# New due times, DMA latency and task costs in the list schedule of a fused attention and SoLU feed-forward kernel

## The chip, the cores and the metric

The kernel runs on one core of a Trainium2 chip. The metric is device time in microseconds (us) of that core; several executions are timed and the median counts. One more execution is taken with the hardware profiler, and all rows shown here come from it.

The core's engines each run their own instruction list in order: TensorE (PE, with its weight loads shown as PEld), VectorE (DVE), ScalarE (ACT), GpSimd (POOL) and SyncE (SP), which here issues nearly all DMAs. Semaphores tie them together, so an instruction that waits holds up all that stands behind it on its engine.

## The reference

```python
scores = scale * np.matmul(q, k.transpose(0, 1, 3, 2))     # q, k, v: 4 x 8 x 768 x 64
...
scores = scores + bias[None, :, :, :]
scores = np.where(keep, scores, -1000000000.0)
...
a = a / (np.sum(a, axis=-1, keepdims=True) + 1e-09)
return np.matmul(a, v).astype(np.float32)
...
h = x @ w_in                                               # x: 3072 x 512, w_in: 512 x 1024
...
solu = h * sm
mu = np.mean(solu, axis=-1, keepdims=True)
var = np.mean((solu - mu) ** 2, axis=-1, keepdims=True)
ln = (solu - mu) / np.sqrt(var + 1e-06) * g_ln
return (ln @ w_out).astype(np.float32)
```

Four batches of eight heads go through attention. A query sees the 96 keys up to itself and the first 8 keys of the sequence; a bias falls with distance. The heads are laid side by side to 3072 tokens of width 512. A feed-forward layer follows: a product with w_in, SoLU (h times its softmax), a layer norm, and a product with w_out. The layer norm's scale cancels the softmax's sum, so that the kernel takes h times exp(h), and w_out is scaled by g_ln and centred ahead of the product.

## The kernel before, in words

Tokens come in 24 tiles of 128, six to a batch. Tile n is numbered through all batches, and token tile n of a batch with a = n mod 6 needs the keys of its own and of the tile before (with a = 0 only its own, and half the work). Every piece of work is a task, added with `add` to a planner (`Plan`, lines 22 to 100). The tasks, by their names in lines 460 to 547:

- `ql`, `qc`, `qt`, `qo`: for each batch, four head pairs and q or k: load (SP, 384 KB), cast to 16 bits (GpSimd, in batch 0 VectorE too), turn (six PE transposes into the PSUM tile pt), and copy in order of tokens (VectorE or ScalarE) into qkT.
- `vl`, `vc`: load and cast of one tile of v (256 KB; GpSimd).
- `s`, `e`, `m`, `av`, each for a half of four heads: scores (PE, tile ps), exponential (ScalarE, eb), mask (VectorE, in place), product with v (PE, tile pav). `gk` and `gv` are GpSimd's copies of the eight global keys and values into the place of the oldest ones, between one tile and the next.
- `n`, `xt`, `xc`: norm by the softmax's sum (VectorE), turn (PE, again a pt), copy to xT (VectorE).
- `h`, `he`, `u`, `ut`, `q`: product with w_in (PE, ph), its exponential (ScalarE), h times exp(h) (VectorE), transposing DMA of u (SP), sum of squares (ScalarE).
- `st`, `pw`, `o`, `os`, `w`: statistics and power (GpSimd) for two tiles, product with w_out (PE, po), scaling (ScalarE or VectorE), store (SP).
- `w_in`, `g`, `wl`, `gr`, `gm`, `gc`: loads of the weights; eight roundings of g times w_out; their mean by one PE product (pm, in po's buffer); eight centrings. No `o` runs before the last `gc`.

The planner places one task at a time. `ready` gives when a task could start on an engine: when the engine is free, its predecessors have ended (with a hop of 0.12 us if on another engine) and a buffer is there. Among the tasks within 0.15 us of the earliest it takes the one with the lowest due time and writes it to the program at once. So the planner's costs and due times set nothing but the order of each engine's list, and which engine does a task that two may do. The buffers (`rooms`, lines 204 to 208) are few in PSUM: one each for ps, pav, pt, ph and po. Before the change, due times are written out task by task in units of T = 5.4, such as

```python
add(("h", n), {"PE": 1.75}, lambda e, n=n: ffn_in(n), s + 1.5 * T,
...
add(("o", n), {"PE": 1.75}, lambda e, n=n: ffn_out(n), s + LAG * T,
```

with s = n T, and LAG = 7. A halved task's second half is due T / 2 later.

Of the kernel before, what the change touches and what calls it, by code (L numbers as in the profile page):

```python
# [21 lines left out]
class Plan:  # L22
# [8 lines left out]

    NEAR = 0.15
    DEEP = 2.5

    def __init__(self, start, hop, rooms):
        self.free = dict(start)
        self.hop = hop
        self.rooms = {r: [0.0] * n for r, n in rooms.items()}
        self.tasks, self.end, self.dma = {}, {}, 0.0

    def add(self, name, engs, emit, due, after=(), takes=(), frees=(), load=0.0, lag=0.0):

        assert name not in self.tasks, name
        self.tasks[name] = (engs, emit, due, tuple(after), takes, frees, load, lag)

    def ready(self, task, eng):
        _, _, _, after, takes, _, load, _ = task
        t = max(self.free[eng], self.dma - self.DEEP) if load else self.free[eng]
        for a in after:
            if a not in self.end:  # L50
                return None
            e, on = self.end[a]
            t = max(t, e + (0.0 if on == eng else self.hop))
# [6 lines left out]
    def run(self):  # L60
        log = []
        left = dict(self.tasks)
        for name, t in left.items():
            for a in t[3]:
                assert a in self.tasks, (name, a)
        while left:
            best = None
            cand = {}
            for name, task in left.items():
                for eng, us in task[0].items():  # L70
                    t = self.ready(task, eng)
                    if t is not None:
                        cand.setdefault(eng, []).append((t, task[2], name, us))
            for eng, c in cand.items():
                t0 = min(x[0] for x in c)
                t, due, name, us = min((x for x in c if x[0] <= t0 + self.NEAR),
                                       key=lambda x: (x[1], x[0]))
                if best is None or (t, due) < best[:2]:
                    best = (t, due, name, us, eng)
            assert best, sorted(left)  # L80
            t, due, name, us, eng = best
            engs, emit, due, after, takes, frees, load, lag = left[name]
            if len(engs) > 1:

                alt = [(x[0] + x[3], e, x[0], x[3]) for e, c in cand.items()
                       for x in c if x[2] == name]
                _, eng, t, us = min(alt)
# [3 lines left out]
            if load:  # L91
                self.dma = done = max(self.dma, done) + load
            done += lag
            for r in frees:
                heapq.heappush(self.rooms[r], done + self.hop)
            self.end[name] = (done, eng)
            log.append((t, us, eng, name))
            del left[name]
# [5 lines left out]
def kernel(  # L104
# [24 lines left out]
    T = 5.4  # L129
    LAG = 7  # L130

# [19 lines left out]
    with tc.manual_schedule():  # L151
# [35 lines left out]
        for h in range(H):  # L187
# [17 lines left out]
            start={"PE": 0.0, ve: 2.0, sc: 8.0, gp: 4.6, "SP": 0.6}, hop=0.12,  # L205
# [254 lines left out]
        add = plan.add  # L460
        BT = NA * T
        for b in range(B):
            for i, (w, pr) in enumerate(PAIRS):
                x = (b, w, pr)
                due = b * BT - (NP * 2 - i) * (0.8 * BT / 8) if b else -40.0 + 2 * i
                add(("ql", *x), {"SP": 0.3}, lambda e, x=x: load_pair(*x), due - 3 * T,
                    takes=("raw",), load=1.1, lag=1.0)
                add(("qc", *x), {gp: 0.86, ve: 0.85} if b == 0 else {gp: 0.86},
                    lambda e, x=x: cast_pair(*x, e), due - 0.5 * T,
                    after=[("ql", *x)], takes=("qkn",), frees=("raw",))  # L470
                last = [("s", NA * (b - 1) - 1, 1)] if b > 1 else []
                add(("qt", *x), {"PE": 0.43}, lambda e, x=x: turn_pair(*x), due,
                    after=[("qc", *x)] + last, takes=("t",), frees=("qkn",))
# [109 lines left out]
```

## Time and profile before

| | us |
|---|---|
| median of three timed runs | 185.64 (185.6 to 186.57) |
| the profiled execution, its time | 186.13 |
| its span, first to last instruction | 184.4 |
| TensorE busy in it | 147.2 |
| ScalarE, VectorE, GpSimd busy | 126.3, 119.1, 79.2 |
| DMA: bytes moved, mean rate | 34.85 MB, 189 GB/s |
| mean granted TensorE clock | 0.954 of full speed |

The span is shorter than the time by what lies around the instructions. An engine's busy time is the sum over its instructions; a row of the timeline gives the start in us, the length, the engine, the source line, the tile written and the tile read, the count, and in brackets the idle time ahead of it with what ended it. In the chain of waits each row is a start, a length and the work that the end of the kernel hung on then.

### The profile page before, as it was taken

How to read it: one execution, taken by the hardware profiler on the slowest of the kernel's cores; microseconds unless marked ns; L12 is line 12 of the kernel's file. 1: busy time of each engine (PE TensorE's matmuls, PEld its weight loads, DVE VectorE, ACT ScalarE, POOL GpSimd, SP SyncE). 2: the span in 40 equal slices, each digit the busy share in tenths (PEclk: the TensorE clock that was granted, in tenths of full speed). 3: DMA queues.
4: the chain of work that ended last, by engine and by line, in shares of the span. 5: the costliest groups of instructions: out<-in, count | busy, mean ns of one | idle time of the engine just before them, and what ended most of it. 6: DMA issues, size and time to landing. Idle time of an engine off the chain costs nothing.

```text
span 184.4 us, 3669 instructions
## 1 busy us (share of the span) xinstructions
PE 147.2 (80%) x1384; PEld 83.1 (45%) x1384; DVE 119.1 (65%) x219; ACT 126.3 (69%) x200; POOL 79.2 (43%) x157
## 2 busy tenths in 40 slices
PE   0337478686779799999999899799998799988581
PEld 0225346244455445555554465555544355444120
DVE  2351466656989996677855887696647677586220
ACT  2827357569984998657668877598787868777401
POOL 7241095357996587154543775350405214020110
PEclk9999999789969999999999999999999999999955
DMA  6999996989999999999999956039243344522731
GB/s 186 320 242 193 322 310 195 244 215 220 282 274 306 237 251 213 334 289 251 334 253 221 264 109 172 0 71 160 57 106 102 88 109 94 139 57 80 114 94 57
DMA packets 65138, 34.85 MB, mean 189 GB/s; under 512 B 52320, under 2 KB 60512, under 8 KB 65120
## 3 DMA queue, kind: packets, MB, share of 16 engines
q1 hardware_dynamic: 64592, 33.57, 74.5%
q0 software_dynamic: 528, 1.05, 3.4%
q8 instruction: 11, 0.18, 0.4%
q14 instruction: 7, 0.06, 0.1%
HBM read 23.07 MB, written 6.29 MB: 159 GB/s over the span
## 4 chain that ended last, share of the span: by engine, by line
PE 52%; DVE 12%; ACT 11%; issue 9%; DMA 6%; POOL 6%; SPq 1%; POOLq 0%
PE ph L349 20%; PE po L406 15%; PE pt L248 5%; PE pav L313 5%; PE ps L275 4%; DVE u L373 4%; DMA raw<-in_k_dram 4%; ACT eb L286 3%; DVE eb L300 3%; ACT qkT L256 3%; DMA uT<-u 2%; DVE qkT L256 2%; ACT sq L383 2%; DVE x L328 2%; ACT e L369 2%
## 5 line engine op out<-in xcount | busy, mean ns | idle before, releaser
L406 PE MATMUL po<-gw_sb,uT 128*128 128x512 f16 x192 | 47.8, 394 | 3.5 <-DMA uT<-u 2.6
L349 PE MATMUL ph<-w_in_sb,xT 128*128 128x512 f16 x192 | 47.6, 393 | 2.0 <-DVE xT L339 1.8
L286 ACT ACTIVATE eb<-ps 128x1024 f16<-128x1024 f32 x40 | 40.8, 1019 | 2.3 <-PE ps L275 2.1
L300 DVE TENSOR_TENSOR eb<-eb,mask 128x1024 f16<-128x1024 f16 (+1 forms) x48 | 34.3, 724 | 9.1 <-ACT eb L290 4.8
L369 ACT ACTIVATE e<-ph 128x1024 f16<-128x1024 f32 x24 | 24.6, 1025 | 21.6 <-PE ph L349 21.6
L373 DVE SCALAR_TENSOR_TENSOR u<-e,ph 128x1024 f16<-128x1024 f16 x24 | 29.1, 1214 | 5.0 <-ACT e L369 5.0
L248 PE MATMUL pt<-ident,qkn 128*128 128x128 f16 x192 | 19.0, 246 | 16.3 <-DVE qkT L256 6.9
L240 POOL CAST qkn<-raw 128x768 f16<-128x768 f32 x26 | 21.8, 847 | 17.1 <-PE pt L248 10.4
L406 PEld LDWEIGHTS <-uT 128*128 128x128 f16 x192 | 17.9, 100 | 24.7 <-DMA uT<-u 4.8
L349 PEld LDWEIGHTS <-xT 128*128 128x128 f16 x192 | 18.0, 101 | 22.7 <-issue 2.7
L383 ACT ACTIVATE sq<-u 128x1024 f16<-128x1024 f16 x24 | 25.4, 1059 | 3.9 <-DVE u L373 3.8
L275 PE MATMUL ps<-qkT 64*128 64x128 f16 x352 | 19.6, 228 | 7.0 <-ACT eb L286 5.5
L248 PEld LDWEIGHTS <-qkn 128*128 128x128 f16 x192 | 15.2, 110 | 21.1 <-issue 8.7
L416 ACT ACTIVATE osb<-po,rs 128x512 f32<-128x512 f32 x18 | 12.4, 686 | 14.3 <-issue 6.4
L313 PE MATMUL pav<-vo,eb 128*128 128x65 f16 x352 | 18.6, 197 | 2.7 <-DVE eb L300 1.5
L256 ACT COPY qkT<-pt 128x768 f16<-128x768 f16 x18 | 14.4, 799 | 8.5 <-PE pt L248 8.5
L222 POOL CAST vo<-vst 128x512 f16<-128x512 f32 x24 | 17.4, 729 | 5.9 <-DMA vst<-in_v_dram 4.0
L256 DVE COPY qkT<-pt 128x768 f16<-128x768 f16 x14 | 13.3, 953 | 9.8 <-PE pt L248 9.8
L226 POOL COPY vo<-vo 8x520 f16<-8x520 f16 x16 | 9.7, 609 | 19.6 <-PE pav L313 19.6
L313 PEld LDWEIGHTS <-eb 128*128 128x128 f16 x352 | 14.8, 100 | 7.2 <-DVE eb L300 4.8
L275 PEld LDWEIGHTS <-qkT 64*128 64x128 f16 x352 | 11.6, 97 | 13.4 <-issue 9.5
L328 DVE TENSOR_TENSOR x<-pav,rl 128x512 f16<-128x512 f32 x24 | 16.6, 692 | 0.8
(49 smaller groups left out, 110.4 us busy)
## 6 DMA issues: line engine op xcount, KB each, us to landing
raw<-in_q_dram SPq DMA_DIRECT2D x16, 384.0 KB, 5.8
raw<-in_k_dram SPq DMA_DIRECT2D x16, 384.0 KB, 5.7
vst<-in_v_dram SPq DMA_DIRECT2D x24, 256.0 KB, 5.0
out_dram<-osb SPq DMA_DIRECT2D x24, 256.0 KB, 2.5
w_out<-in_moe_w_out_dram SPq DMA_DIRECT2D x4, 512.0 KB, 5.0
w_in_sb<-in_moe_w_in_dram POOLq DMA_DIRECT2D x1, 1024.0 KB, 9.8
uT<-u SPq DMA_TRANSPOSE x24, 3.4
g_sb<-in_moe_g_ln_dram SPq DMA_DIRECT2D x1, 4.0 KB, 8.3
```

What stands on the lines that cost most here:

```text
L240: ENG[eng](out=t.rearrange("p a m d -> p m a d"), in_=raws.pop((b, w, pr)).rearrange("p m (a d) -> p m a d", d=D))
L248: nc.tensor.transpose(out=pt[:, a, :], in_=src[:, a].rearrange("p m d -> p (m d)"), identity=ident)
L256: ENG[eng](out=dst, in_=pts.pop((b, w, pr)).rearrange("p a t -> p t a"))
L275: nc.tensor.matmul(out=ps[:, m, slot, blk, :], lhsT=qkT[b][r, NP + pr, ts(a - blk, P)], rhs=qkT[b][r, pr, ts(a, P)], start=True, stop=True)
L286: nc.scalar.activation(out=eb.rearrange("p m s b f -> p (m s b f)"), in_=ps.rearrange("p m s b f -> p (m s b f)"), func=AF.Exp, scale=inv_ ...
L300: nc.vector.tensor_tensor(out=eb.rearrange(pat), in0=eb.rearrange(pat), in1=mk.rearrange(pat if n % NA else "p m s f -> p (m s f)"), op=AL ...
L313: nc.tensor.matmul(out=pav[:, half, ds(i * (D + 1), D + 1)], lhsT=eb[:, m, slot, blk, :], rhs=vo[:, b % 2, a - blk, 4 * half + i, :], star ...
L349: nc.tensor.matmul(out=ph[:, ds(fh * 512, 512)], lhsT=xT[:, j, :], rhs=w_in_sb[:, j, ds(fh * 512, 512)], start=(j == 0), stop=(j == NCC - 1))
L369: nc.scalar.activation(out=es[n], in_=phs[n], func=AF.Exp, accum_out=acc)
L373: nc.vector.scalar_tensor_tensor(out=us[n], in0=es.pop(n), scalar=1.0, in1=phs.pop(n), op0=ALU.mult, op1=ALU.mult, accum_out=sums(n, 1))
L383: nc.scalar.activation(out=sq, in_=us[n], func=AF.Square, scale=D_FF ** -0.5, accum_out=sums(n, 2))
L406: nc.tensor.matmul(out=po, lhsT=uT[:, c, :], rhs=gw_sb[:, c, :], start=(c == 0), stop=(c == NFC - 1))
```

## The change

The planner takes new numbers, and is told more of DMA.

- A task's due time is now T (n + D + i S), with T = 4.34, n its tile (a batch's first tile for q/k), i the half, pair or part, and D and S two numbers for its kind from a table of some 70. Batch 0, batch 1 and batches 2 and 3 have q/k kinds of their own (`ql0`, `ql1`, `ql2` and so on).
- A DMA reaches the engines 1.2 us after its issue (`SENT`) and its data are seen 0.9 us after it has landed (`SEEN`); these stand in place of a lag given with each task.
- Costs are changed by some hundredths to tenths (a turn of q/k 0.43 to 0.36, a cast of v 0.63 to 0.73, an exponential of ph 1.12 to 1.18).
- A rounding of w_out may no longer go to GpSimd, and the load of w_in no longer waits for batch 0's last cast.
- A tie between equal due times falls to the task added first.

Buffers, tiles, instructions and the arithmetic are as they were. The diff, cut:

```diff
-    def __init__(self, start, hop, rooms):
+    HOP = 0.12
...
+    SENT, SEEN = 1.2, 0.9
...
             if load:
-                self.dma = done = max(self.dma, done) + load
-            done += lag
+                self.dma = max(self.dma, done + self.SENT) + load
+                done = self.dma + self.SEEN
...
-    T = 5.4
+    T = 4.34
...
+    DUE = {
+        "ql0": -140.45, "ql0+": 3.00, "qc0": -5.55, "qc0+": 2.05, "qt0": -71.06,
...
+        "u": -79.84, "ut": -29.51, "q": -24.86, "st": -18.75, "pw": 97.28, "o": 77.23,
...
+        def due(what, n, i=0):
+
+            return T * (n + DUE[what] + i * DUE.get(what + "+", 0.0))
...
-                add(("av", n, h), {"PE": 0.13 if z else 0.26}, lambda e, n=n, h=h: av(n, h),
-                    sh + 0.5 * T,
-                    after=[("m", n, h), ("vc", n)] + ([("av", n, 0)] if h else [])
...
+                add(("av", n, h), {"PE": 0.15 if z else 0.28}, lambda e, n=n, h=h: av(n, h),
+                    n, h, after=[("m", n, h), ("vc", n)] + ([("av", n, 0)] if h else [])
...
-        add("w_in", {gp: 1.2}, lambda e: load_w_in(), -37.0, load=5.4, lag=1.0,
-            after=[("qc", 0, 1, 1)])
...
+        add("w_in", {gp: 1.2}, lambda e: load_w_in(), 0, load=5.4)
...
-            add(("gr", j), {sc: 0.62, ve: 0.62, gp: 0.75}, lambda e, j=j: gw_round(j, e),
...
+            add(("gr", j), {sc: 0.72, ve: 0.74}, lambda e, j=j: gw_round(j, e), 0, j,
```

What this does to the order is seen in the built programs. First GpSimd's list while the fourth tile is worked on; st and rs belong to the layer norm's statistics, gw_sb is the rounded w_out, vo the cast v, qkn a cast pair of q or k. Before:

```order
L260 COPY qkT<-qkT 128x4x8
L400 TENSOR_TENSOR rs<-vs,nhalf 128x2
L222 CAST vo<-vst 128x8x64
L444 TENSOR_SCALAR gw_sb<-w_out_69,g_sb 128x512 x2
L226 COPY vo<-vo 8x520
L240 CAST qkn<-raw 128x2x6x64
```

The same place in the changed program (source lines are 12 higher there):

```order
L234 CAST vo<-vst 128x8x64 x2
L238 COPY vo<-vo 8x520
L412 TENSOR_TENSOR rs<-vs,nhalf 128x2
L234 CAST vo<-vst 128x8x64 x2
L252 CAST qkn<-raw 128x2x6x64 x2
L403 TENSOR_TENSOR t_829<-st 128x4
```

The two roundings of w_out are gone from GpSimd, which casts v further ahead; ScalarE does five and VectorE three of the eight, and pm, which needs all of them, moves on TensorE from just ahead of the fifth h to between the first and the second. On SyncE the four loads of w_out move from among batch 1's loads to just behind v's first tile.

Second, TensorE's list late in the program, matrix products alone, with the buffers' numbers; ps are scores, pav the product with v, eb the exponentials (masked in place), xT the turned input of ph. Before, where eb2_2233 and eb2_2273 are the exponentials of ps_2197 (the scores ahead of this piece) and of ps_2252:

```order
L406 MATMUL po_2236<-gw_sb_71,uT_2168 128x512
...
L275 MATMUL ps_2252<-qkT_1558 128x128
...
L313 MATMUL pav_2263<-vo_67,eb2_2233 128x65
...
L349 MATMUL ph_2275<-w_in_sb_68,xT_2245 128x512
...
L313 MATMUL pav_2263<-vo_67,eb2_2273 128x65
```

In the changed program, where eb2_2131 and eb2_2182 are the exponentials of ps_2100 and ps_2143:

```order
L287 MATMUL ps_2195<-qkT_1377 128x128
...
L361 MATMUL ph_2204<-w_in_sb_68,xT_2171 128x512
...
L287 MATMUL ps_2236<-qkT_1377 128x128
...
L325 MATMUL pav_2245<-vo_67,eb2_2131 128x65
...
L325 MATMUL pav_2245<-vo_67,eb2_2182 128x65
...
L418 MATMUL po_2265<-gw_sb_71,uT_2034 128x512
```

Before, a product with v follows its own scores by one or two groups; now ps_2143, ps_2195 and ps_2236 stand between ps_2100 and the product with its exponentials.

Third, the end of TensorE's list; uT is the transposed u that the product po with w_out reads. Before:

```order
L349 MATMUL ph_2528<-w_in_sb_68,xT_2517 128x512
...
L406 MATMUL po_2566<-gw_sb_71,uT_2513 128x512
...
L349 MATMUL ph_2591<-w_in_sb_68,xT_2584 128x512
...
L406 MATMUL po_2611<-gw_sb_71,uT_2586 128x512
...
L406 MATMUL po_2637<-gw_sb_71,uT_2622 128x512
```

And in the changed program:

```order
L418 MATMUL po_2544<-gw_sb_71,uT_2366 128x512
...
L361 MATMUL ph_2565<-w_in_sb_68,xT_2522 128x512
...
L418 MATMUL po_2582<-gw_sb_71,uT_2457 128x512
...
L418 MATMUL po_2601<-gw_sb_71,uT_2524 128x512
...
L418 MATMUL po_2625<-gw_sb_71,uT_2574 128x512
...
L418 MATMUL po_2637<-gw_sb_71,uT_2612 128x512
```

The products with w_out now lag by four tiles from the start (the first one stands ahead of the fifth ph) to the end, where four follow the last ph; before, the first stood behind the seventh ph, they caught up, and two followed the last.

More of the change, by code (lines that the diff above doesn't have):

```diff
@@ L464 @@
                 x = (b, w, pr)
[L465 to L471, printed above, removed]
@@ new lines @@
+                add(("pw", g), {gp: 0.7}, lambda e, g=g: ffn_pow(g), n, after=[("st", g)])
+            add(("o", n), {"PE": 1.75}, lambda e, n=n: ffn_out(n), n,
+                after=[("ut", n)] + [("gc", j) for j in range(NFC)], takes=("o",),
+                frees=("uT",))
+            add(("os", n), {sc: 0.7, ve: 0.75}, lambda e, n=n: scale_out(n, e), n,
+                after=[("o", n), ("pw", g)], takes=("osb",), frees=("o",))
+            add(("w", n), {"SP": 0.5}, lambda e, n=n: store(n), n,
+                after=[("os", n)], frees=("osb",), load=0.75)
```

149 lines of the change are left out of this document (74 added, 75 removed), and 9 rows, old and new, of the table DUE.

## The prediction

> **What bounds the kernel now.** I read the page first, then the stages by windows, then the chain of waits in the densest stretch, then TensorE's timeline for the starts of single tasks.
>
> ```profile
> span 184.4 us, 3669 instructions
> PE 147.2 (80%) x1384; PEld 83.1 (45%) x1384; DVE 119.1 (65%) x219; ACT 126.3 (69%) x200; POOL 79.2 (43%) x157
> ```
>
> ```profile
> 0.00:26.10 26.10, 10.83 (x99) 7.99 (x100) 10.91 (x19) 13.50 (x27) 10.55 (x28) 1.00 0.97 256
> 26.10:56.60 30.50, 23.23 (x258) 14.31 (x257) 21.88 (x39) 23.44 (x35) 20.87 (x33) 0.89 0.97 248
> 56.60:169.10 112.50, 105.04 (x1007) 58.22 (x1005) 83.25 (x153) 85.36 (x132) 46.66 (x95) 1.00 0.74 171
> 169.10:184.40 15.30, 8.08 (x24) 2.59 (x24) 3.08 (x12) 4.03 (x8) 1.10 (x2) 0.67 0.41 87
> ```
>
> Each window gives length, busy time of PE, PEld, DVE, ACT, POOL, the granted clock, the DMA share and GB/s. The borders are mine: 26.1 is the start of token tile 0's first FFN product (h0), 56.6 that of h4, 169.1 that of the last, h23. Until h4 the DMA is full (0.97) and PE is not; then PE is; the end is a thin chain at a clock of 0.67.
>
> Busy time overstates PE's work, since pipelined matmuls overlap. The chain of waits shows what a task takes from start to start:
>
> ```profile
> 74.54 1.73 PE po L406 x8
> 76.26 0.22 PE pt L335 x4
> 76.49 0.24 PE pav L313 x8
> 76.73 0.33 PE ps L275 x8
> 79.13 1.73 PE ph L349 x8
> 80.86 0.35 PE pt L248 x6
> ```
>
> So o and h are 1.73 us each, a q/k turn (qt) 0.35, a half's scores 0.33, its av 0.24, a turn of x (xt) 0.22; halves of a batch's first tile take half. All 24 tiles need 24 x (2 x 1.73 + 2 x 0.33 + 2 x 0.24 + 0.22) - 2.3 for the four short tiles + 32 x 0.35 + 1.83 for the mean (gm): 126 us of the 184.4. The other 58 are waits and a slow clock. The Trainium skill, Perfetto Trace Analysis, section Identifying the Most-Contended Engine, says the same of matmul busy time: no measure of the distance to the roofline. By busy time the third window could lose at most 112.5 - 105.0 = 7.5 us.
>
> Where the waits lie follows from the starts of h1, h4, h6, h13, h16 and h23 on TensorE's timeline:
>
> ```profile
> 34.90 3.34 PE L349 MATMUL ph<-w_in_sb,xT 128*128 128x512 f16 x8 [1.09 <-DVE xT L339]
> 56.62 1.89 PE L349 MATMUL ph<-w_in_sb,xT 128*128 128x512 f16 x8
> 65.54 1.89 PE L349 MATMUL ph<-w_in_sb,xT 128*128 128x512 f16 x8
> 115.02 1.89 PE L349 MATMUL ph<-w_in_sb,xT 128*128 128x512 f16 x8
> 131.60 1.89 PE L349 MATMUL ph<-w_in_sb,xT 128*128 128x512 f16 x8
> 169.16 1.90 PE L349 MATMUL ph<-w_in_sb,xT 128*128 128x512 f16 x8 [0.52 <-DVE xT L339]
> ```
>
> I counted the tasks between these in the program's order and priced them as above. h6 to h13: 46.2 us of work in 49.5 (93%); there a backlog of thirteen o's filled every gap. h16 to h23: 31.9 in 37.6 (85%). h4 to h23 as a whole: 98.4 in 112.5.
>
> **The change part by part.** Instructions stay nearly the same; what moves is order. ScalarE gets one more q/k copy and two more roundings of gw and loses two output scalings; VectorE gets two scalings and one cast and loses one copy; GpSimd loses two roundings and a cast. Rows for these and for the loop through ph:
>
> ```profile
> L369 ACT ACTIVATE e<-ph 128x1024 f16<-128x1024 f32 x24 | 24.6, 1025 | 21.6 <-PE ph L349 21.6
> L369 ACT ACTIVATION_READ_ACCUMULATOR e<-ph 128x1 f32 x24 | 4.8, 200 | 0.0
> L373 DVE SCALAR_TENSOR_TENSOR u<-e,ph 128x1024 f16<-128x1024 f16 x24 | 29.1, 1214 | 5.0 <-ACT e L369 5.0
> L418 DVE TENSOR_SCALAR osb<-po,rs 128x512 f32<-128x512 f32 x6 | 4.5, 750 | 5.6 <-issue 2.8 <-PE po L406 1.7 <-POOL vo L222 1.1
> L441 ACT ACTIVATE gw_sb<-w_out,g_sb 128x512 f16<-128x512 f32 x3 | 2.2, 723 | 0.0
> L444 POOL TENSOR_SCALAR gw_sb<-w_out,g_sb 128x512 f16<-128x512 f32 x2 | 3.3, 1643 | 0.0
> ```
>
> VectorE's net is under 2.1 us on 119 (two scalings at 0.75 and a cast of 0.56, in a row below, less a copy), ScalarE's 0.9 on 126 (a copy of 0.81, below, and 2 x 0.72 - 2 x 0.69; its scalings last 0.69 in the last row of this part). Neither engine is full in any window, so I cost them at nothing; where VectorE or ScalarE is late, it is late for the reasons priced below. The planner's new code runs on the host: nothing.
>
> *Up to h4.* Three things change. First, the early q/k chain. VectorE's second copy stood behind a cast that waited 2.93 us for a load; ScalarE now takes that copy. After it the chain is paced by one turn (cold, 0.81) and one copy (0.81) through the single buffer t:
>
> ```profile
> 9.37 0.56 DVE L240 CAST qkn<-raw 128x768 f16<-128x768 f32 x1 [2.93 <-DMA raw<-in_k_dram]
> ```
>
> ```profile
> 11.68 0.81 ACT qkT L256
> 12.53 0.81 PE pt L248 x6
> ```
>
> That is about 1 us gained: h0 at 25.3. Second, GpSimd's two roundings go; they stood in the chain between h3 and h4:
>
> ```profile
> 46.95 3.27 POOL gw_sb L444 x2
> ...
> 54.95 1.83 PE pm L451 x8
> ```
>
> Third, all of w_out is loaded ahead of v1 and batch 1, and gm goes between h0 and h1. There it waits on PE for the eighth rounding, with the scores and q/k turns of what follows queued behind it. Walked by these durations: h0 ends at 27.8, its exponential (1.03, and 0.2 for reading its sum) and two roundings (1.45) hold gm to 30.4, PE idles 2 us, gm ends at 32.2, three turns with their copies and two score exponentials put h1 at 37; then 4.4, 5.1 and 6.0 us, the last with o0 inside, give h4 at 52.5. The short ones are the loop h, exponential, u, h through the single ph: 1.73 + 1.2 + 1.25 and hops. The walk has a full clock after h0 and lets no load be late. The window above has a clock of 0.89 and 248 GB/s, and batch 1's first pair is due on PE at 32.6 when it has been there for only about 2 us. I add 2.5: **h4 at 55.0**. Bounds: 52.5, and 60.4 if the old gap stays (56.6 + 2.1, by which h1 moves from 34.9 to 37, + 1.73 for o0).
>
> *From h4 to h23.* In after's order 19 h, 19 o, 29 full and 4 half scores, 30 full and 5 half av's, 19 xt and 15 qt stand there: 93.2 us, 5.2 less than now, since three o's lie elsewhere. The spacing of scores and av is the larger point. Now av follows its scores by one other task group and PE waits for ScalarE, then VectorE; in the new order three more score halves stand between. Going by hand through h6 to h9 with the durations above I find 15.3 us for 15.2 of work: exponential, square, mask, u and copy each end before PE asks. Such a walk leaves out late loads, so I take the best rate that PE has shown, 93.4%: 93.2 / 0.934 = 99.7. Bounds: 97% (96.0) and 84.8% (109.8). The DMA must keep up until all inputs are in. The rows of its largest loads, with KB each:
>
> ```profile
> raw<-in_q_dram SPq DMA_DIRECT2D x16, 384.0 KB, 5.8
> ...
> vst<-in_v_dram SPq DMA_DIRECT2D x24, 256.0 KB, 5.0
> ```
>
> Six tiles need 8 x 384 + 18 x 256 KB (v, uT, out) = 7.9 MB, at 250 GB/s 31.4 us, 5.2 per tile. PE's pace would be 99.7 / 19 = 5.25: they are level, so slack is what was loaded ahead.
>
> *From h23 to the end.* Now two o's follow h23, then four:
>
> ```profile
> 173.33 2.61 PE L406 MATMUL po<-gw_sb,uT 128*128 128x512 f16 x8 [2.27 <-DMA uT<-u]
> 176.83 3.57 PE L406 MATMUL po<-gw_sb,uT 128*128 128x512 f16 x8 [0.90 <-DVE osb L418]
> ```
>
> ```profile
> 180.49 0.69 ACT L416 ACTIVATE osb<-po,rs 128x512 f32<-128x512 f32 x1 [5.84 <-issue]
> ```
>
> The wait of 2.27 for the last transposes is covered by o20 and o21. But po is one buffer, so each o waits for the scaling of the one before: 1.75 (h23) + 4 x 1.73 + 3 x 0.85 + 0.3 for the end of the last, then 0.75 and the 3.2 us that now lie between the last scaling and the end: 15.5, against 15.2 now. This takes a full clock. In the rows the clock is halved in the last o (3.57 for 8); if it halves after o20 here too, three o's cost 1.75 more each: 20.7. I take the full clock, as the gaps are 0.85 and not 2.27. The Trainium skill, TensorE: Matmul & The Clock Gate, section Why this matters for your kernels, asks for gaps under about 3 us; here the clock fell after 2.27. By its rule this end stays at 15.5.
>
> **Sum.** 55.0 + 99.7 + 15.5 = 170.2 us of span. The profiled execution took 186.13 for a span of 184.4; the median, 185.64, is 1.2 above the span. So 171.4, say **171**.
>
> **The rivals.**
>
> *The pace stays.* Single buffers (s, t, ph, po) tie the engines whatever the order, and PE runs at 84.8% as it did from h16 to h23: 55.0 + 109.8 + 15.5 + 1.2 = 181.5. For it: the 83 and 85 us that VectorE and ScalarE are busy in the third window would be 83 and 86% of 99.7, in strict order. Against: the waits there were for av's mask, which now has time. 0.25.
>
> *Loads come late: slower.* GpSimd's queue is first in, first out, and the casts of v and q/k stand in it ahead of the copies of the global keys and values, for which scores and av wait. Where a cast waits for its load, PE waits too.
>
> ```profile
> POOL qkn L240 <- DMA raw<-in_q_dram: 5.3, 3, 3.2
> ...
> POOL vo L222 <- DMA vst<-in_v_dram: 4.0, 5, 1.5
> ```
>
> ```profile
> L222 POOL CAST vo<-vst x24: 606/616/1096, 14.3 to 111.7; 128x512 f16<-128x512 f32 x24
> ```
>
> The last v is cast at 111.7 now, at the latest that DMA allows; the new order would be at tile 14 by then. If PE waits 1.5 us (the longest for v) at each of the 15 tiles till then, 171.4 + 22.5 = 193.9; it is slower than before from 1.0 us a tile. Against: loads run dry only if SP waits for a u with loads behind it. 0.09.
>
> *It does nothing.* The old gap before h4 stays (60.4), PE keeps 87.4% (106.6), the end stays: 60.4 + 106.6 + 15.5 + 1.2 = 183.7, or 188.9 with the slow clock at the end. 0.05.
>
> **How the numbers follow.** The forecast has 0.54 (its own range 165 to 178: 52.5 + 96.0, and 57 + 104.9 at 88.8%, the rate of h4 to h16); better than 165 has 0.07. Faster by over 0.5%, about what a measurement of this kernel can tell: 0.54 + 0.07 + 0.25 = 0.86; same 0.05; slower 0.09. All likely cases have one sign. A range from 165 to 184 leaves out the better end (0.07), late loads (0.09) and the half of the last case that lies above 184: under 0.2.
>
> **What the new profile would show.** Right: h4 near 55 with one o done; about 5.25 us from h to h after it, PE near 9 tenths throughout; no rounding on GpSimd; four o's after h23 with gaps near 0.85 at full clock. Wrong: GpSimd's casts waiting for DMA by tens of us in all; PE waiting for VectorE or ScalarE between scores and av; a clock under 0.8 in the last window; h1 past 40 because gm waits for w_out.

## The result, and the profile after

| | median, us | runs | span of the profiled run, us |
|---|---|---|---|
| before | 185.68 | 4 (185.6 to 186.57) | 184.4 |
| after | 170.01 | 4 (169.84 to 170.58) | 168.1 |

The ratio is 0.916 (95% interval 0.912 to 0.919). The 171 us of the prediction lies 1 us above it, and the range of 165 to 184 holds it. The three terms of the sum, from the starts of h4 and h23 on TensorE's timeline:

| | before | predicted | after |
|---|---|---|---|
| up to h4 | 56.6, no o | 55.0, one o | 52.35, one o |
| h4 to h23 | 112.5, 22 o's | 99.7, 19 o's | 99.64, 19 o's |
| h23 to the end | 15.2, two o's | 15.5, four o's | 16.1, four o's |

First the page, which answers to the first two rows shown of before:

```profile
span 168.1 us, 3666 instructions
PE 142.3 (85%) x1384; PEld 78.7 (47%) x1384; DVE 118.4 (70%) x221; ACT 127.3 (76%) x201; POOL 73.8 (44%) x154
```

Then the windows between the same events, with the same columns (length, PE, PEld, DVE, ACT, POOL, granted clock, DMA share, GB/s):

```profile
0.00:24.90 24.90, 10.76 (x100) 7.74 (x100) 9.86 (x19) 15.45 (x30) 6.53 (x23) 1.00 1.00 281
24.90:52.30 27.40, 24.38 (x267) 14.22 (x266) 24.22 (x45) 23.62 (x36) 18.16 (x29) 1.00 0.97 249
52.30:152.00 99.70, 97.92 (x983) 53.03 (x984) 81.81 (x151) 82.13 (x127) 48.05 (x100) 1.00 0.84 192
152.00:168.10 16.10, 9.28 (x40) 3.71 (x39) 2.48 (x10) 6.08 (x10) 1.10 (x2) 0.96 0.52 116
```

Two numbers answer to the old windows. In the second, the column of the clock reads 1.00 and read 0.89; how far that column can be trusted there is said at the end. In the third, PE is busy for 97.9 of 99.7 us and was for 105.0 of 112.5. What ended PE's waits there is a list of two; before, the same stretch had seven kinds. First after, then before (engine, line, what it waited for, us in total, times, longest):

```profile
PE ph L361 <- DVE u L385: 0.9, 2, 0.7
PE ps L287 <- POOL qkT L272: 0.8, 2, 0.4
```

```profile
PE ps L275 <- ACT eb L286: 2.9, 6, 0.8
PE pt L335 <- DVE x L328: 1.2, 2, 1.0
PE pav L313 <- DVE eb L300: 0.9, 2, 0.5
PE ph L349 <- DVE xT L339: 0.7, 2, 0.5
PE pt L248 <- DVE xT L339: 0.5, 1, 0.5
PE pt L335 <- DVE qkT L256: 0.4, 2, 0.2
PE po L406 <- DMA uT<-u: 0.3, 1, 0.3
```

The longest of the old waits is that of scores for the exponential of the scores before them (L286), which has to read the single buffer ps first; the wait of av for the mask (L300) is 0.9 of 6.9 us.

So the 12.9 us that the middle lost are made up as follows. Three o's lie elsewhere: 5.2, at 1.73 each. The idle times in the rows of TensorE's timeline there, up to the start of h23, fell from 6.9 to 1.7: 5.2. The remaining 2.5 is work that takes less from one start to the next, av above all: that of a single half took 0.33 us on average and takes 0.26. The end, on TensorE's timeline (start, length, idle before and what ended it):

```profile
151.99 1.89 PE L361 MATMUL ph<-w_in_sb,xT 128*128 128x512 f16 x8 [0.74 <-DVE u L385]
153.72 1.89 PE L418 MATMUL po<-gw_sb,uT 128*128 128x512 f16 x8
156.43 1.89 PE L418 MATMUL po<-gw_sb,uT 128*128 128x512 f16 x8 [0.83 <-ACT osb L428]
159.09 1.89 PE L418 MATMUL po<-gw_sb,uT 128*128 128x512 f16 x8 [0.78 <-ACT osb L428]
162.12 1.90 PE L418 MATMUL po<-gw_sb,uT 128*128 128x512 f16 x8 [1.14 <-DMA uT<-u]
```

Four o's at full clock, two gaps as predicted, and a third of 1.14 that was longer and ended by a transpose, not by a scaling.

The terms of the experiments below come from the one profiled run of each kernel; for two of them (the due times alone, and o ahead of h) it took 2.7 and 4 us more than the shortest of its kernel, and the ratios, unlike the medians, leave out runs over 1.5% longer than the shortest.

### The profile page after: what moved, and what is told of

The parts are those of the page before. It is cut to its first block, busy times and chain, and to the rows that moved or that the text cites. A ratio compares the mean times of both kernels' runs of the same rounds, so it can differ in the third digit from the quotient of the medians.

```text
span 168.1 us, 3666 instructions
## 1 busy us (share of the span) xinstructions
PE 142.3 (85%) x1384; PEld 78.7 (47%) x1384; DVE 118.4 (70%) x221; ACT 127.3 (76%) x201; POOL 73.8 (44%) x154
## 4 chain that ended last, share of the span: by engine, by line
PE 44%; DMA 26%; SPq 16%; POOL 6%; issue 4%; DVE 2%; ACT 1%; POOLq 0%; ACTq 0%
PE ph L361 16%; PE po L418 14%; DMA raw<-in_k_dram 10%; DMA vst<-in_v_dram 6%; SPq L229 6%; SPq L245 6%; PE ps L287 5%; DMA uT<-u 5%; PE pav L325 5%; DMA raw<-in_q_dram 4%; SPq L447 3%; POOL qkn L252 3%; PE pt L260 2%; PE pt L347 2%; POOL vo L234 2%
## 5 line engine op out<-in xcount | busy, mean ns | idle before, releaser
L418 PE MATMUL po<-gw_sb,uT 128*128 128x512 f16 x192 | 45.3, 379 | 2.7 <-ACT osb L428 1.6
L312 DVE TENSOR_TENSOR eb<-eb,mask 128x1024 f16<-128x1024 f16 (+1 forms) x48 | 32.8, 693 | 6.1 <-ACT eb L302 4.0
L252 POOL CAST qkn<-raw 128x768 f16<-128x768 f32 x25 | 21.0, 840 | 14.7 <-DMA raw<-in_q_dram 8.6
L234 POOL CAST vo<-vst 128x512 f16<-128x512 f32 x24 | 16.5, 691 | 19.6 <-DMA vst<-in_v_dram 19.2
L260 PEld LDWEIGHTS <-qkn 128*128 128x128 f16 x192 | 14.0, 107 | 16.4 <-issue 7.4
L428 ACT ACTIVATE osb<-po,rs 128x512 f32<-128x512 f32 x16 | 11.0, 684 | 11.1 <-PE po L418 8.3
L268 ACT COPY qkT<-pt 128x768 f16<-128x768 f16 x19 | 15.2, 801 | 5.4 <-PE pt L260 5.2
L325 PE MATMUL pav<-vo,eb 128*128 128x65 f16 x352 | 16.7, 196 | 0.2 <-POOL vo L234 0.2
L268 DVE COPY qkT<-pt 128x768 f16<-128x768 f16 x13 | 12.4, 955 | 5.8 <-PE pt L260 5.8
L412 POOL TENSOR_TENSOR rs<-vs,nhalf 128x2 f32<-128x2 f32 (+1 forms) x13 | 8.9, 685 | 14.9 <-DVE vs L407 14.5
L325 PEld LDWEIGHTS <-eb 128*128 128x128 f16 x352 | 13.1, 99 | 3.1 <-issue 0.8
```

The source lines that it names most:

```text
L252: ENG[eng](out=t.rearrange("p a m d -> p m a d"), in_=raws.pop((b, w, pr)).rearrange("p m (a d) -> p m a d", d=D))
L260: nc.tensor.transpose(out=pt[:, a, :], in_=src[:, a].rearrange("p m d -> p (m d)"), identity=ident)
L268: ENG[eng](out=dst, in_=pts.pop((b, w, pr)).rearrange("p a t -> p t a"))
L312: nc.vector.tensor_tensor(out=eb.rearrange(pat), in0=eb.rearrange(pat), in1=mk.rearrange(pat if n % NA else "p m s f -> p (m s f)"), op=AL ...
L325: nc.tensor.matmul(out=pav[:, half, ds(i * (D + 1), D + 1)], lhsT=eb[:, m, slot, blk, :], rhs=vo[:, b % 2, a - blk, 4 * half + i, :], star ...
L418: nc.tensor.matmul(out=po, lhsT=uT[:, c, :], rhs=gw_sb[:, c, :], start=(c == 0), stop=(c == NFC - 1))
```

## The experiments

The theory at the start: the order that the new due times make carries the gain, by an o beside each h and by more work between scores and av; the rest of the change is calibration. The rivals: the DMA model and true costs are the gain, or GpSimd's rounding was what held the front. The table has medians of four runs or more, ratios to the kernel before on the same chip, and the terms, in us, with the number of o's in the last two. The diffs stand against the changed kernel, where nothing else is said.

| kernel | us | ratio (95%) | up to h4 | h4 to h23 (o's) | end (o's) |
|---|---|---|---|---|---|
| after | 170.01 | 0.916 (0.912 to 0.919) | 52.35 | 99.6 (19) | 16.1 (4) |
| due times alone | 176.59 | 0.949 (0.935 to 0.963) | 56.9 | 102.3 (20) | 15.7 (4) |
| all but due times | 185.78 | 1.003 (0.999 to 1.006) | 57.1 | 113.1 (22) | 13.3 (2) |
| before, GpSimd rounds nothing | 189.92 | 1.031 (1.021 to 1.041) | 52.2 | 122.7 (22) | 13.3 (2) |
| after, GpSimd rounds | 175.11 | 0.937 (0.928 to 0.945) | 54.3 | 102.1 (20) | 15.7 (4) |
| after, old DMA model | 177.74 | 0.952 (0.945 to 0.959) | 55.1 | 99.9 (18) | 21.2 (6) |
| three exponential buffers | 182.15 | 0.984 (0.974 to 0.994) | 53.2 | 100.7 (16) | 27.0 (8) |
| priority by kind | 190.92 | 1.033 (1.024 to 1.041) | 74.6 | 98.4 (18) | 16.2 (4) |
| one set for q/k | 171.98 | 0.923 (0.915 to 0.931) | 52.1 | 101.9 (19) | 16.1 (4) |
| o ahead of h | 184.47 | 0.987 (0.976 to 0.998) | 53.0 | 115.6 (21) | 15.0 (2) |
| half a v tile more | 179.74 | 0.972 (0.965 to 0.978) | 54.6 | 106.9 (19) | 16.5 (4) |
| half of v | 169.72 | 0.909 (0.902 to 0.916) | 52.7 | 98.3 (19) | 15.7 (4) |
| end in two banks | 167.56 | 0.906 (0.899 to 0.912) | 52.4 | 99.1 (19) | 13.4 (4) |

### Which part carries the gain

**Due times alone.** The table, with the costs, the DMA model and the choice of engines as before:

```diff
-    SENT, SEEN = 1.2, 0.9
+    LAGS = {"ql0": 1.0, "ql1": 1.0, "ql2": 1.0, "vl0": 1.0, "vl": 1.0, "ut": 1.5, "w": 1.5,
...
-            add(("gr", j), {sc: 0.72, ve: 0.74}, lambda e, j=j: gw_round(j, e), 0, j,
+            add(("gr", j), {sc: 0.62, ve: 0.62, gp: 0.75}, lambda e, j=j: gw_round(j, e), 0, j,
```

> The new table of due times alone: the old task costs, the old DMA model with its lags, GpSimd still offered the rounding, the load of w_in still behind the last cast of the first q/k batch. Theory: the order is the whole gain. I expect 169 to 173 us, the stretch from h4 to h23 at 99 to 102 us with an o after almost every h, and the end within 1 us of the changed kernel's 16.1. Rival (the DMA latency in the plan keeps the new order from issuing transposes and loads too late): 176 to 181 us, with PE waiting for the transposed u or for GpSimd's casts by some us in all between h4 and h23.

Measured 176.59 us (174.13 to 177.19). The middle and the end are as expected, 102.3 and 15.7, so the order does carry the larger part: 5.1 points of 8.4 (3.7 to 6.5 by the interval). But h4 comes 4.6 us later than in the changed kernel, with o0 not yet done; 1.8 us of that are h1 and h3 at a lower clock (3.33 and 2.27 us for 1.89). The rival had the right size and the wrong place: between h4 and h23 PE waits little.

**All but due times.** The complement; the due times come from the old formulas:

```diff
+        OLD = 5.4
+        def due(what, n, i=0):
+            s, b, t = n * OLD, n // NA, OLD
...
+            if what in ("s", "e", "m", "av"):
+                return s + i * t / 2 + {"s": 0.0, "e": 0.1, "m": 0.2, "av": 0.5 * t}[what]
```

> Everything of the change but the table: the new DMA model and latency, the new task costs, no rounding on GpSimd, w_in not tied to a cast; the due times come from the old formulas, with the old 5.4 us per tile. Theory: without the table the order stays that of before (attention and h keep their places, pm near h4, the o's some eight tiles behind until late), so 181 to 187 us with 109 to 113 us from h4 to h23. Rival (the plan was merely badly calibrated, and true costs and latencies would have given the gain with the old due times): 172 to 176 us.

Measured 185.78, ratio 1.003: no change, as the theory had it. The new costs and latencies do nothing for the old due times. With the new ones all that is not the table is worth the other 3.3 points. The next three runs ask what of it; no run has the new costs alone, or the earlier load of w_in alone.

**GpSimd without the rounding, in the kernel before.** Against the kernel before:

```diff
-            add(("gr", j), {sc: 0.62, ve: 0.62, gp: 0.75}, lambda e, j=j: gw_round(j, e),
+            add(("gr", j), {sc: 0.62, ve: 0.62}, lambda e, j=j: gw_round(j, e),
```

> The kernel before, with one edit: GpSimd is no longer offered the rounding of w_out, so ScalarE and VectorE do all eight; its due times, costs and DMA model stay the old ones. Theory (the order carries the gain): the rounding on GpSimd is at most a matter of the first 57 us, and h4 cannot come before pm, which stays behind it in this order; I expect 182 to 186 us, h4 between 54 and 57, the stretch from h4 to h23 at 112 us as before. Rival (the GpSimd rounding held up pm, and with it everything up to h4): h4 comes at 52 to 53 as in the changed kernel and the time is about 181. A time under 178 would refute both.

Measured 189.92: slower by 3%, which no theory had. h4 does come at 52.2, since gm now stands behind it; but the middle takes 10 us more. 1.7 of them are gm itself. PE's idle rows there come to 9.6 us for 6.9, of which 2.8 are waits for VectorE's masks; VectorE now does five of the eight roundings and did three. And the clock falls after short waits. TensorE's timeline in this run, around h6:

```profile
62.86 0.38 PE L335 MATMUL pt<-ident,x 128*128 128x128 f16 x4 [1.23 <-ACT qkT L256]
63.79 0.40 PE L275 MATMUL ps<-qkT 64*128 64x128 f16 x8 [0.54 <-ACT eb L286]
64.94 0.41 PE L313 MATMUL pav<-vo,eb 128*128 128x65 f16 x8 [0.76 <-DVE eb L300]
65.28 3.36 PE L349 MATMUL ph<-w_in_sb,xT 128*128 128x512 f16 x8
```

Three waits, none above 1.23 us, and h6 takes 3.36 us for 1.89: half the clock. h4 takes 3.44, so the two cost 3 us. The Trainium skill, TensorE: Matmul & The Clock Gate, section A second HAM failure mode: psum-queue depth-cycling, tells of a kernel in which PE idles briefly and often between groups of matmuls and its clock goes down and up again and again; the 3.36 us after these three waits agree.

**GpSimd with the rounding, in the changed kernel.**

```diff
-            add(("gr", j), {sc: 0.72, ve: 0.74}, lambda e, j=j: gw_round(j, e), 0, j,
+            add(("gr", j), {sc: 0.72, ve: 0.74, gp: 0.75}, lambda e, j=j: gw_round(j, e), 0, j,
```

> The changed kernel, with GpSimd offered the rounding of w_out again (at the old 0.75 us); the order then gives it four of the eight, early, between the copies of the global keys and the casts of v. In the run with the due times alone GpSimd had three of them, 1.56 to 1.78 us each, and h4 came at 56.9 and not at 52.4. Theory (the rounding on GpSimd made those 4.6 us): h4 at 55 to 58, 173 to 176 us, with GpSimd's casts late and the rest as in the changed kernel. Rival (the loss came from the old DMA model or the old costs): h4 at 52 to 53.5, 170 to 171.5 us.

Measured 175.11, as the theory expected; h4 at 54.3 is a little below its bounds, and o0 is not yet done there, which is 1.8 us more. The roundings by engine in this run (ns min/median/max, first and last start):

```profile
L456 POOL TENSOR_SCALAR gw_sb<-w_out,g_sb x4: 1555/1646/1745, 21.9 to 27.1; 128x512 f16<-128x512 f32 x4
L456 DVE TENSOR_SCALAR gw_sb<-w_out,g_sb x2: 479/562/646, 25.1 to 26.8; 128x512 f16<-128x512 f32 x2
```

The planner is told 0.75 us and GpSimd takes 1.65, so four of them take 3.6 us more than the plan allows. The first cast of q/k behind them starts at 31.87, and at 28.47 in the changed kernel. The order differs in other places too (h1 comes at 34.3 and not at 37.1), so how much of the loss is this queue is not split up.

**The old DMA model in the changed kernel.**

```diff
-                self.dma = max(self.dma, done + self.SENT) + load
-                done = self.dma + self.SEEN
+                self.dma = done = max(self.dma, done) + load
+            done += self.LAGS.get(name if isinstance(name, str) else name[0], 0.0)
```

> The changed kernel with the old model of a DMA in the planner (a fixed lag behind the load, no time to be sent): new due times, new costs, no rounding on GpSimd. The order then lets o0 come two tiles later and leaves six o's behind h23. Theory (the model decides where the o's stand, not when the front is done): h4 within 1.5 us of 52.4, 1.8 us less for each o that is missing up to h23, 2.7 us more for each behind it: 171.5 to 174 us. Rival (the model is what e2's front lacked): h4 at 55 to 58 and 175 to 179 us.

Measured 177.74: the rival, in place and size (e2 is the run with the due times alone). The front shows how. The plan believes that a load is there sooner than it is, and puts a cast that waits for it ahead of a copy that PE waits for. VectorE, then TensorE in this run:

```profile
9.56 0.56 DVE L253 CAST qkn<-raw 128x768 f16<-128x768 f32 x1 [2.50 <-DMA raw<-in_k_dram]
10.04 0.95 DVE L269 COPY qkT<-pt 128x768 f16<-128x768 f16 x1
```

```profile
11.04 0.80 PE L261 MATMUL pt<-ident,qkn 128*128 128x128 f16 x6 [3.12 <-DVE qkT L269]
```

This is the row of before that the prediction quoted (a cast waiting 2.93 us), back again; h0 comes at 26.7 and not at 24.9, 1.8 of the 2.8 us by which h4 is late. Another 5.1 us are at the end, where six o's stand behind h23 and not four. My theory, that the model only places the o's, fell; its price of 2.7 us for each o at the end about held, with 5.1 for two.

### What the order does

**Three exponential buffers.**

```diff
-                   "qkn": 4, "eb": 4, "x16": 2, "xT": 3, "e": 3, "u": 5, "ut": 5, "uT": LAG + 1,
+                   "qkn": 4, "eb": 3, "x16": 2, "xT": 3, "e": 3, "u": 5, "ut": 5, "uT": LAG + 1,
```

> The changed kernel, with the planner told that there are three buffers of exponentials and not four, so that the product with v can stand fewer score halves behind its scores; the buffers themselves are unchanged. By the same due times the order then leaves eight o's behind h23, not four. Theory (depth between scores and the product with v, and an o beside each h, are what took the waits away): the stretch from h4 to h23 loses three to four o's of 1.85 us (92 to 94 us if no wait comes), and waits for VectorE's masks come back by 2 to 6 us; the end takes 23 to 25 us in place of 16.1; in all 172 to 178 us. Rival (depth does not matter, the waits were those of the old order): 169 to 171 us, no PE idle row for the mask above 1 us in all.

Measured 182.15, 4 us above the theory's range and 11 above the rival's. The end is the larger part: 27.0 us, since each o behind h23 costs 2.73 us through the single po (10.9 more for four). In the middle three o's less (1.79 each, as measured in the changed kernel) should have given 94.3 and it took 100.7: 6.4 us of waits and slower steps came back, a little more than expected; 4.1 of them are idle rows. They are not the expected ones. The longest four of nine kinds:

```profile
PE ph L361 <- DVE u L385: 1.9, 4, 0.8
PE pav L325 <- POOL vo L238: 1.6, 1, 1.6
PE pt L260 <- DVE xT L351: 0.8, 2, 0.6
PE pt L260 <- ACT qkT L268: 0.6, 2, 0.3
```

No wait for the mask is in the list, so that depth helps by giving the mask time, as I had argued, is not borne out. That depth is what was lost here is not shown either. Counted on TensorE's timeline from h4 to h23, the score halves that stand between a half's scores and its av are 1.0 on average before, 2.0 in the changed kernel and 1.4 in this run; but they are 1.4 in the next run too, whose idle rows come to 1.7 us there as in the changed kernel, against 5.8 here. This run also has fewer o's to fill the middle, 16 for 19. Its loss has no single cause that is shown.

**Priority by kind.**

```diff
+        RANK = {w: r for r, w in enumerate(sorted((w for w in DUE if w[-1] != "+"),
+                                                  key=lambda w: DUE[w]))}
-            return T * (n + DUE[what] + i * DUE.get(what + "+", 0.0))
+            return 1000.0 * RANK[what] + 10.0 * n + i
```

> The changed kernel, with the due time replaced by the rank of the kind in the table (the kind with the lowest number first), then the tile, then the part; the steps and the 4.34 us per tile are gone. Theory: the table's numbers lie so far apart (from -165.81 to 97.28 tiles, and there are 24) that they act as a list of priorities and no more; I expect 168 to 174 us, the o's still one to an h. Rival (the distances and the steps are what was tuned): 176 us or more, with waits of PE between h4 and h23 of over 3 us.

Measured 190.92: the theory fell, but not where the rival said. The middle is as fast as ever (98.4 us with 18 o's). The front is 22 us later, and two rows show why. In the table the later q/k loads (9.08 and 9.34) and the v loads (12.95) lie close, so the tile's number decides between them; by rank the q/k loads go first. SyncE's queue and TensorE in this run:

```profile
45.05 0.37 SPq L245 DMA_DIRECT2D raw<-in_k_dram  x1
45.69 12.02 SPq L229 DMA_DIRECT2D vst<-in_v_dram  x7
```

```profile
55.02 1.04 PE L325 MATMUL pav<-vo,eb 128*128 128x65 f16 x16 [10.95 <-POOL vo L234]
```

v1 is issued at 45.7 and not at 14.6, behind 22 loads of q and k more, and PE stands still for 10.95 us. So on PE from h4 on the table acts as a list of priorities, and on the load queue its distances decide. The 4.34 us order nothing in the changed kernel, since they multiply every due time alike.

**One set of numbers for q/k.**

```diff
-                k_ = str(min(b, 2))
+                k_ = str(min(b, 1))
```

> The changed kernel with one set of numbers for the q/k batches 1, 2 and 3: the last two take those of batch 1, so that their transposes no longer come ahead of nearly everything and no longer wait until the last scores of the batch before. The order up to h6 hardly changes; transposes of the last two batches stand up to three earlier in the rows of PE. Theory (with room for four cast pairs, and the same loads, it hardly matters): 169.5 to 172 us. Rival (own numbers for the later batches are a part of the gain): 174 to 180 us, with PE waiting for scores or transposes between h8 and h20.

Measured 171.98, the upper end of the theory; the interval overlaps the changed kernel's. The middle is 2.2 us longer, with one wait of 1.7 for the global keys. Own numbers for the later batches are worth some 2 us in this run, and that much is not settled.

**o ahead of h.**

```diff
-        "u": -79.84, "ut": -29.51, "q": -24.86, "st": -18.75, "pw": 97.28, "o": 77.23,
+        "u": -79.84, "ut": -29.51, "q": -24.86, "st": -18.75, "pw": 97.28, "o": 40.00,
```

> The changed kernel with one number of the table changed: o from 77.23 to 40.00, so that o comes ahead of h (44.73) when both could run; two o's are left behind h23 and not four. Theory (o is the work that PE has in reserve, and is best kept back): between h4 and h23 stand two o's more (99.6 + 2 x 1.83 = 103.3 us) and PE waits for the transposed u by 1 to 4 us; the end is as long as in the kernel before, which also had two o's there (15.2 us); in all 172 to 176 us. Rival (the end is what four o's cost, 16.1 us, and falls to 12.5 with two): 167 to 170 us.

Measured 184.47 (181.27 to 185.34): the direction of the theory, 8 us above its range. The end is the expected 15.0, with the last o at half clock (3.60 us after a wait of 1.01, and one of 2.27 before it). The middle took 115.6 for the expected 103.3 plus 1 to 4. The idle rows come to 11.0 us there, for 1.7 in the changed kernel. Besides 3.2 us for the transposed u, PE waits at eleven other kinds of place; the longest four of the list:

```profile
PE po L418 <- DMA uT<-u: 3.2, 5, 1.0
PE ps L287 <- POOL qkT L272: 2.2, 1, 2.2
PE pt L260 <- DVE xT L351: 1.0, 3, 0.5
PE pt L260 <- DVE qkT L268: 0.8, 1, 0.8
```

Four o's go between h4 and h5, which come 17.5 us apart; after that no o is in reserve to fill a gap. The idle rows and the two o's make 12.9 of the 15.9 us more; where the rest goes is open.

### What bounds the kernel now

**Half a v tile more.**

```diff
+    more = const.tile([P, N_TOK // P, 4, D], FP32, name="more")
...
+            nc.sync.dma_start(out=more[:, n], in_=v[b, 0:4, ts(a, P), :].rearrange("h p d -> p h d"))
```

> The changed kernel with 24 loads more, one of 128 KB beside each tile of v, into a buffer that nobody reads: 3.15 MB on top of 34.85 MB. The output is unchanged. In the prediction the DMA of a tile (5.2 us) was level with PE's work (5.25 us). If DMA bounds the first 105 us, in which its share is 9 tenths and more, then 3.15 MB at the 260 GB/s of those windows is 12 us, and the time goes to 178 to 184 us. If PE bounds from h4 on and DMA only up to h4: up to 52 us some 12 of the 24 loads are issued, 1.6 MB or 6 us at 260 GB/s; 173 to 178 us. If DMA bounds nowhere: 170 to 171 us, only the issue time on SyncE.

Measured 179.74: the case in which DMA bounds the first 105 us. 9.8 us of span for 3.15 MB, 7.2 of them between h4 and h23. PE waits there for copies that stand in GpSimd's queue behind casts that wait for loads. First PE's waits, then GpSimd's queue ahead of the longest of the six (PE waits 1.50 us for the copy at 61.24):

```profile
PE ps L289 <- POOL qkT L274: 5.7, 6, 1.5
PE pav L327 <- POOL vo L240: 1.5, 1, 1.5
```

```profile
60.47 0.83 POOL L254 CAST qkn<-raw 128x768 f16<-128x768 f32 x1 [0.82 <-DMA raw<-in_k_dram]
61.24 0.21 POOL L274 COPY qkT<-qkT 128x32 f16<-128x32 f16 x1
```

**Half of v.**

```diff
-            vst[n] = sb.tile([P, H, D], FP32, name="vst", bufs=4)
+            vst[n] = sb.tile([P, H // 2, D], FP32, name="vst", bufs=4)
...
-            ENG[eng](out=vo[:, b % 2, a, :, 0:D], in_=vst.pop(n))
+            twice = bass.AP(tensor=t.tensor, offset=t.offset,
+                            ap=[t.ap[0], [0, 2], [D, H // 2], [1, D]])
```

> The changed kernel with only heads 0 to 3 of each tile of v loaded, and cast twice in their place; heads 4 to 7 of v are left out, 3.15 MB of 34.85 less. All other instructions are unchanged. With 3.15 MB more the span grew by 9.8 us, 7.2 of them between h4 and h23. If PE is already at its floor between h4 and h23, that stretch stays at 98 to 100 us and only the front falls, by up to 5 us: 165 to 169 us. Rival (DMA still sets the pace there, and PE's work only fills it): the stretch falls to 92 to 96 us, 158 to 163 us in all.

Measured 169.72 (168.48 the profiled run, span 166.7). The middle takes 98.3, 1.3 less, with no wait but 0.9 for u: PE is at its floor there, and the rival fell. The front did not fall either (52.7), against what I expected: v is not what it waits for. So 3.15 MB less give 1.4 us and 3.15 MB more cost 9.8: DMA and PE are level, which is what the prediction said of them (5.2 and 5.25 us a tile).

### The end

**In two banks.**

```diff
-            po = pos[n] = psum.tile([P, D_MODEL], FP32, name="po", tag="o")
+            if n in AVS:
+                po = pos[n] = psum.tile([P, 2, 512], FP32, name="pav", tag="av")[:, 0]
...
-                after=[("os", n)], frees=("osb",), load=0.75)
+                after=[("os", n)] + ([("ut", NT - 1)] if n > NT - 5 else []),
+                frees=("osb",), load=0.75)
```

AVS holds 21 and 23; their o's also wait for h23 in the plan.

> The changed kernel with another end: o21 and o23 accumulate in the PSUM buffer that the attention has left by then, so that o20 to o23 need not wait for the scaling of the one before, and the last transpose of u is issued ahead of the store of o20. Reasons read from the changed kernel's end: o21 and o22 wait 0.83 and 0.78 us for ScalarE's scaling, o23 waits 1.14 us for the transposed u, whose issue stands behind a store and takes 2.63 us where others take 1.2 to 1.3. If these are the bounds: u23 is there at 156.3, transposed 3.4 us later at 159.7, o23 ends 161.5, the last store 3.9 us later as now (168.1 - 164.2), so a span of 165.5 to 166.2 and 167 to 168 us, 0.980 to 0.989 of the changed kernel's 170.0. Rival (the transpose takes as long wherever it is issued, as four loads of one kind end together at the end): 169.3 to 170 us.

Measured 167.56 (166.64 to 171.53), the span 164.9, of which the end is 13.4 and was 16.1. SyncE issues the last transpose at 155.84, in 1.23 us, and it lands 3.05 us after its start; in the changed kernel it was issued at 156.84, in 2.63, and o23 started 5.3 us later. TensorE in this run:

```profile
154.97 1.89 PE L422 MATMUL pav<-gw_sb,uT 128*128 128x512 f16 x8
156.82 1.90 PE L422 MATMUL po<-gw_sb,uT 128*128 128x512 f16 x8
158.94 1.90 PE L422 MATMUL pav<-gw_sb,uT 128*128 128x512 f16 x8 [0.22 <-DMA uT<-u]
```

Of the three gaps 0.22 us is left, and the span is a little below the 165.5 expected. The ratio to the kernel before is 0.906 for 0.916; the two intervals just miss each other (0.912). So this version is faster than the kernel before and, by about 1%, probably than the changed kernel.

## Why the prediction was right

The sum was 170.2 us of span, and 168.1 came. Up to h4 2.65 us were too many and at the end 0.6 too few. The last term, 1.2 from span to time, was taken between the median and a profiled run that was longer than the median; from one run's span to its own time it is 1.7 in both kernels.

**Up to h4 (55.0; measured 52.35).** The walk came out right and the allowance on top of it wrong. h0 was put at 25.3 and came at 24.93, h1 at 37.0 and came at 37.10, h4 by the walk at 52.5. Between h0 and h1 two errors cancelled: h0 took 3.60 us where the walk has 2.5, and gm began at 29.44 where the walk holds it to 30.4. The step that failed is "I add 2.5" for a slow clock and late loads. Both were taken from the old window (0.89, 248 GB/s). The GB/s stayed at 249, but in the idle rows between h0 and h4 only 0.23 us are a wait for GpSimd's casts. And the clock, read from the lengths of the large products, cost little after h0: gm took 2.28 us for 1.89, h1 to h3 took 1.89 to 1.90; in the old order h1 had taken 3.34. That the denser order kept the clock is the reading that fits and is not shown; what is certain is that a clock can't be carried over from the old order.

**GpSimd's rounding.** "GpSimd's two roundings go" was costed as one wait less. By itself it is no gain: in the old order taking it away cost 3%. In the new order it is worth 2 points. The run with it put back has GpSimd's casts 3.4 us late, so that the queue behind the rounding matters, and not the one wait, is likely; the run does not separate it from the other moves in the order.

**h4 to h23 (99.7; measured 99.64).** The number was right, its two factors each off. The work of the tasks is 97.9 (99.64 less the 1.7 of idle rows) and not 93.2: from one start to the next on the timeline, less the idle rows, a turn of x takes 0.30 on average and not 0.22, an o 1.79, a q/k turn 0.37. PE fills 98% of the stretch, not 93.4%. The errors cancelled, since the rate was taken from before with the same too low prices; that the term agrees to 0.1 us is luck. The direction of the reason, fewer waits by another order, is borne out: the table of due times alone brings the middle to 102.3, and the rest of the change alone leaves it at 113.1. The details are not. "Three more score halves stand between" is the largest number; it is three for ten of 35 halves and two on average, one before. "The waits there were for av's mask" holds for 0.9 of 6.9 us; the largest part was the scores' wait for the exponential. And neither the run with three buffers nor another one isolates the depth: orders with 1.4 halves between have 1.7 and 5.8 us of idle rows. What the runs do show is that an o kept in reserve matters: brought ahead of h, the idle rows are 11.0 us.

**DMA level with PE.** Shown by the two runs that add and remove 3.15 MB.

**The end (15.5; measured 16.1).** Full clock, gaps of 0.83 and 0.78 for the 0.85 taken. The step that failed is "the wait of 2.27 for the last transposes is covered by o20 and o21": the cover was there, but the last transpose stood behind a store, and the third gap was 1.14. From start to start the o's took 2.71, 2.66 and 3.03 us where the sum has 2.58.

**The signs.** Those called right came, but for h4, which came earlier. One of those called wrong did occur: GpSimd's casts waited for DMA by tens of us.

```profile
POOL vo L234 <- DMA vst<-in_v_dram: 19.2, 10, 9.8
...
POOL qkn L252 <- DMA raw<-in_q_dram: 8.6, 7, 2.2
...
POOL qkn L252 <- DMA raw<-in_k_dram: 5.0, 6, 2.3
```

32.8 us, and PE waited 1.0 us for GpSimd in all. The sign should have been PE's wait for the copies behind those casts, which is what 3.15 MB more brought out. Of the rivals, "the pace stays" and "it does nothing" are refuted by the middle and by h4. "Loads come late" did not happen, but it was near: 9% more bytes take back 9.8 of the 16.3 us.

**What I had not foreseen** is that the parts hang together: the table alone gives 5.1 points, the rest alone none, both 8.4. Nor do they add up: taken out of the changed kernel one at a time, the choice of engine for the rounding costs 2.1 points and the DMA model 3.6, more than the 3.3 that all but the table brings.

## What to carry to other kernels

A list schedule is as good as its latencies: with a load believed too early, or an engine believed twice as fast as it is, the planner puts a wait at the head of a queue where others need it. In this kernel truer numbers in turn did nothing without the right priorities. Keep one long task that depends on little as the filler for each step, let it trail by as many steps as the end can hide, and look at the end as a stage of its own (a second PSUM buffer and one transpose issued earlier were worth 2.7 us of it here). When two resources come out level in the working, add and remove a tenth of one: a cost when it is added and hardly a gain when it is removed says that the other one bounds, with little room.

## What the runs showed of the hardware

- The granted clock halved after three waits of 0.5 to 1.2 us within 4 us, with no long one among them (h6 in 3.36 us, in the run of before without GpSimd's rounding), and stayed full through gaps of 0.8 to 1.1 us between o's of 1.73 at the end of the changed kernel. One gap's length alone did not decide it.
- The granted clock reads 1.00 in the window from 24.9 to 52.3 of the changed kernel, and h0 at its start took 3.60 us for 1.89. In this case the clock of the first 30 us is read from a task's length, not from that column.
- Scaling and rounding 128 x 512 from f32 to f16 took 1.65 us on GpSimd and 0.56 on VectorE. The Trainium skill, GPSIMD Engine Reference, section Engine selection, has GpSimd near line rate for operations with one input; this measurement differs, and decides for this operation. A plain cast of the same size took GpSimd 0.62 us (the median for vo in the kernel before).
- The transposing DMA of 256 KB was issued in 1.23 us and landed 3.05 us after its start with no store just ahead of it; 0.4 us behind a store of 256 KB its issue took 2.63 us. It was seen at this one place with its two sides, so the store as the cause is likely and not shown.
